# Part of a weight piece kept in a PSUM bank, a new step order, and the last stores moved off GpSimd

## The chip, the core and the metric

The kernel runs on one core of one Trainium2 chip. The core has TensorE (PE, matrix products; its weight loads are shown as PEld), VectorE (DVE), ScalarE (ACT), GpSimd (POOL) and SyncE (SP), which here only issues DMAs. The engines run side by side, each through its own instructions in order, and wait for each other through semaphores. Sixteen DMA engines move data between DRAM and the on-chip memory (SBUF). PE writes its results to PSUM, which has eight banks of 2 KB on each of 128 partitions. The metric is the device time of one execution in microseconds (us); lower is better.

## The reference

Two independent results stand side by side in the output. Part A is a sliding-window attention over 2048 rows. Part B, which takes most of the time, is a recurrence: 64 segments of 32 rows, each with 8 memory rows that the segment before has made.

```python
for s in range(n_seg):                                # 64 segments
    h = jnp.concatenate([mem, xs], axis=1)            # 8 memory rows + 32 rows, 640 wide
    q = jnp.einsum('btd,dhe->bhte', h, Wq)            # 32 heads of 192: 640 -> 6144
    k = jnp.einsum('btd,dhe->bhte', h, Wk)
    v = jnp.einsum('btd,dhe->bhte', h, Wv)
    scores = jnp.einsum('bhqe,bhke->bhqk', q, k) * scale
    p = _softmax(jnp.where(mask, scores, -1e9))
    o = jnp.einsum('bhqk,bhke->bhqe', p, v)
    o = jnp.einsum('bhte,hed->btd', o, Wo)            # 6144 -> 640
    mem = o[:, :M, :]                                 # the next segment needs this
    outs.append(o[:, M:, :])
```

The four weights of part B have 640 x 6144 numbers each, 31 MB in bf16 together, and every segment uses all of them. They do not fit into SBUF, which is why some of them are read again in each segment.

## The kernel before

Part A runs first. While it runs, SP loads those weights of part B that stay in SBUF (the resident units) and copies the others into contiguous pieces in DRAM (`copy_streamed`, the tensors `wcopy_*`).

Part B works in units. A unit of Wq, Wk or Wv, `(m, g, dc)`, serves one of four groups `g` of heads and one fifth `dc` of the 640 inputs; it has 1536 columns on 128 partitions, 384 KB. A unit of Wo, `("o", i, 0)` with i from 0 to 23, has 1280 columns, 320 KB, in four quarters of 320 columns. The table `STREAMED` names the units that are not resident. They come through `fetch`, which takes the next slot of a ring of seven (`nbuf=7`, `wstream`, the tile `t` in the profile) and lets SP issue one DMA from `wcopy_*`. SP runs through its DMAs in program order and waits for a slot until PE has used the unit that was in it, so it is as far ahead of PE as the seven slots allow.

One segment is a list of steps, `ORDER` (for the first segment `FIRST`). Steps of all engines stand in one list, and each of PE, DVE, ACT and SP executes its part of it in exactly this order:

- `q.g`, `k.g`, `v.g`: PE projects the segment (line 562; 20 matmuls, or 40 when the late rows are renewed as well, which happens to one k and one v group in each segment). The result lies in one of three banks `acc`.
- `e.q0` and so on: the result is copied to QT or KT by the engine that `EVACUATE` names for it (S is ACT, V is DVE; lines 568, 601); `T.q0`: DVE transposes it in place (572) and GpSimd fills in eight columns. `ve.g` copies v to `Vst` (615), always on ACT. QT, KT and Vst exist once.
- `S.g`: scores on PE (626) into one of the banks `px`; `sb`, `mx`, `sub`, `send`: the softmax on DVE, with the exponential on ACT (632 to 658), in that bank until `send` is done.
- `tp.g`, `PT.g`: PE transposes the probabilities into a `px` bank (665), ACT or DVE spreads them (`SPREAD`; 673, 676). `mix.g`: the product with v (689), into two `px` banks. `ot.g`: both are copied to OT (697) by the engines that `HEADS` names, and GpSimd stores the late rows' part.
- `out.g.0`, `out.g.1`: four and two units of Wo for groups 0 to 2 (714), accumulated in Y. `part` and `join` add the halves of Y (721, 726). `last`: the six units of group 3 (740). `close`: DVE writes the memory rows of the next segment and the output tile XS. `ql`, `eql`, `Tql`: the late rows' q of the next segment.
- At each step named in `STORE_AT`, SP issues one of the four stores of XS of the segment before. `ve.2` also issues the load of the next XS, and `tx` turns it.

In the profile, PE's order in a segment is q0 k0 k1 q1 S0 v0 q2 S1 k2 tp0 v1 q3 mix0 tp1 S2 k3 out0 (first part) v2 out0 (second part) mix1 S3 tp2 v3 mix2 out1 tp3 out2 mix3 last ql.

PSUM's eight banks in part B: three `acc`, four `px` and one for Y.

After the last segment, `project_late` multiplies the late rows of all segments, which GpSimd has stored as `late_o` (16 blocks of 384 KB), by Wo. It uses all eight banks as sums: first for the blocks m = 0 and 1, then for 2 and 3. `head` is the first ten resident units of Wo, `tail` the rest. SP loads `late_o` with `load_late` into the dead q units, four blocks during the last segment and the others later. `store` copies a sum to SBUF by ACT and DVE (871) and then stores eight strided row groups by SP, GpSimd and ACT in turn (876). Behind everything stands the program's end, in which each engine drains; its instructions carry the line number 986.

Of the kernel before, what the change touches and what calls it, by code (L numbers as in the profile page):

```python
# [23 lines left out]
def part_a(ctx, tc, A_x, A_wqkv, A_wo, out, ident, emit_loads):  # L24
# [241 lines left out]
    with tc.manual_schedule(engines={mybir.EngineType.PE, mybir.EngineType.DVE, mybir.EngineType.Activation}):  # L266
# [4 lines left out]
        for b in range(-1, n_blk):  # L271
# [12 lines left out]

STREAMED = {"q": ((), (), (), ()), "k": ((1, 3), (1, 2), (0, 2), (1, 3)), "v": ((0, 1, 4), (2, 4), (0, 2, 4), (0, 2)),
            "o": (8, 12, 17, 19, 23)}
PARTS = {}
# [4 lines left out]
    q.0 e.q0 T.q0 k.0 e.k0 T.k0 q.1 S.0 sb.0 e.q1 T.q1 k.1 mx.0 sub.0 e.k1 T.k1 send.0 v.0 ve.0 S.1 sb.1  # L292
    q.2 e.q2 tp.0 PT.0 T.q2 k.2 e.k2 T.k2 mx.1 sub.1 mix.0 ot.0 v.1 ve.1 send.1 S.2 sb.2 out.0.0 out.0.1
    tp.1 mx.2 sub.2 PT.1 q.3 e.q3 T.q3 k.3 send.2 e.k3 T.k3 mix.1 ot.1 v.2 ve.2 tp.2 PT.2 out.1.0 S.3
    sb.3 mx.3 sub.3 out.1.1 mix.2 ot.2 send.3 v.3 ve.3 out.2.0 tp.3 PT.3 tx out.2.1 part mix.3 ot.3 join
    ql eql last close Tql
# [12 lines left out]
LEAD_IN = 114  # L309
# [10 lines left out]
def part_b(ctx, tc, B_x, B_mem0, B_Wq, B_Wk, B_Wv, B_Wo, out, ident, n_seg, pre, nbuf, mid):  # L320
# [8 lines left out]

    def streamed(u):  # L330
        return u[1] in STREAMED["o"] if u[0] == "o" else u[2] in STREAMED[u[0]][u[1]]

# [28 lines left out]
    def quarter(w, u, i):  # L361

        n = quarter_cols(u)
        if isinstance(w, tuple):
            now = PARTS[u]
            v = w[0][:, n * i:n * i + n] if i < now else w[1][:, n * (i - now):n * (i - now) + n]
            return v.rearrange("p (b c) -> p b c", b=2) if u[0] == "o" else v
        if u[0] == "o":
            return w[:, 640 * (i // 2):640 * (i // 2) + 640].rearrange("p (b g c) -> p g b c", b=2, g=2)[:, i % 2]
        return w[:, n * i:n * i + n]  # L370

    def stream_cols(u):
        return quarter_cols(u) * PARTS.get(u, 4)

# [5 lines left out]
    def copy_streamed():  # L380

        for m, g in need:
            for u in pieces(m, g):
                if u in PARTS:
# [79 lines left out]
    ps_acc = pool("b_ps_acc", bufs=3, space=PSUM)  # L464
    ps_x = pool("b_ps_x", bufs=4, space=PSUM)
    ps_y = pool("b_ps_y", bufs=1, space=PSUM)
    respool2 = pool("b_res2", bufs=1)
    place_resident(respool2, resident[n_pre + len(early):])
    wait.update(resident[n_pre + len(early):])

    fetched = {}

    def fetch(u):
        t = wstream.tile([128, SLOT], BF16, tag="ws")
        nc.sync.dma_start(t[:, 0:stream_cols(u)], copied[u])
        return t[:, 0:stream_cols(u)]

# [280 lines left out]
    def segment(s):  # L758
# [90 lines left out]
    def project_late():  # L849
# [18 lines left out]
        def store(m):  # L868
# [5 lines left out]
            for n in range(M):  # L874
                queue = (nc.sync, nc.gpsimd, nc.scalar if m == 3 and n < 6 else nc.sync)[n % 3]
                queue.dma_start(dst[SEG - M + n], rows[n:128:M])
# [114 lines left out]
```

## Time and profile before

| what | value |
|---|---|
| median of 3 runs | 1866.58 us (1863.11 to 1874.28) |
| the profiled execution: its own time | 1876.93 us |
| its span, first to last instruction | 1875.0 us |
| mean granted TensorE clock | 0.986 |
| busy time of PE, DVE, ACT, POOL | 1649.2, 1288.8, 683.8, 556.9 us |
| moved by DMA | 627.62 MB, mean 335 GB/s |

The profile covers one execution. A group row names the line, the engine, the operation, what is written and read, the shapes and the count, then the busy time and the mean duration in ns, and then the idle time of the engine just before these instructions with what ended it. A row of the timeline has the start, the length, the engine, the line, the operation and the count; in brackets stands the idle time before it and what ended it. A row of the table of waits gives the total, the number of times and the longest. A row of the DMA issues gives the size and the median time from issue to landing. Matmuls are pipelined and their ends are modelled, so a short wait of PE can be hidden inside its busy time.

### The profile page before, as it was taken

What the parts mean: (1) busy time and instruction counts of PE and PEld (TensorE: products, weight loads), DVE (VectorE), ACT (ScalarE), POOL (GpSimd) and SP (SyncE); (2) the same over time, 40 slices, a digit from 0 to 9 for tenths busy, and PEclk for the clock granted to TensorE, in tenths of its full rate; (3) what the DMA queues carried; (4) which work ended last, traced back from release to release, by engine and by line L of the source; (5) the groups of instructions that cost most, each with busy time, mean ns of one, the idle gap of its engine ahead of it and who ended that gap; (6) DMA issues with size and microseconds to landing.
All of it is one profiled execution on the core that took longest, in us unless ns stands there. A gap on an engine that the chain in (4) does not pass through costs nothing.

```text
span 1875.0 us, 91432 instructions
## 1 busy us (share of the span) xinstructions
PE 1649.2 (88%) x39286; PEld 1043.2 (56%) x39286; DVE 1288.8 (69%) x3671; ACT 683.8 (36%) x1821; POOL 556.9 (30%) x1624
## 2 busy tenths in 40 slices
PE   8998898888998888888899889888988888899887
PEld 5565555555555555555555555555555555455567
DVE  4786676767777777776777767776777777677730
ACT  3454333333333333333333333333333333333310
POOL 3001233333333333332333333233333333333311
PEclk9998999999999999999999999999999999999999
DMA  9925999999999999999999999999999999999980
GB/s 327 321 72 196 377 358 354 351 350 360 369 368 351 365 358 363 344 362 357 343 360 366 356 347 358 358 351 344 364 354 362 354 361 351 326 366 351 353 336 24
DMA packets 277858, 627.62 MB, mean 335 GB/s; under 512 B 64116, under 2 KB 76898, under 8 KB 277452
## 3 DMA queue, kind: packets, MB, share of 16 engines
q1 hardware_dynamic: 266668, 610.37, 91.0%
q0 software_dynamic: 10720, 11.36, 1.8%
q8 instruction: 308, 5.05, 1.1%
q14 instruction: 98, 0.80, 0.1%
q10 hardware_dynamic: 64, 0.04, 0.0%
HBM read 607.47 MB, written 22.91 MB: 336 GB/s over the span
## 4 chain that ended last, share of the span: by engine, by line
PE 51%; DMA 27%; DVE 10%; issue 5%; ACT 4%; SPq 1%; POOL 0%; ACTq 0%; DVEq 0%; POOLq 0%
PE acc L562 26%; DMA t<-wcopy_v 22%; PE Y L714 6%; PE px L626 4%; PE px L740 3%; PE pq L95 3%; PE px L689 3%; DMA t<-wcopy_k 3%; PE px L863 1%; DMA t<-wcopy_o 1%; ACT OT L697 1%; PE po L161 1%; ACT QT L721 1%; PE px L665 1%; PE acc L863 1%
## 5 line engine op out<-in xcount | busy, mean ns | idle before, releaser
L562 PEld LDWEIGHTS <-HX 128*32 128x32 bf16 x19380 | 503.1, 96 | 384.0 <-issue 156.8
L562 PE MATMUL acc<-t,HX 128*32 128x384 bf16 x5812 | 434.7, 329 | 65.4 <-DMA t<-wcopy_v 43.0
L562 PE MATMUL acc<-wres_q,HX 128*32 128x384 bf16 x6460 | 324.3, 328 | 14.1 <-issue 12.3
L562 PE MATMUL acc<-wres_k,HX 128*32 128x384 bf16 x3876 | 270.6, 327 | 9.8 <-issue 8.2
L698 POOL COPY OL<-OT 128x96 bf16<-128x96 bf16 x256 | 159.5, 623 | 266.3 <-ACT OT L697 171.8
L562 PE MATMUL acc<-wres_v,HX 128*32 128x384 bf16 x3232 | 215.9, 330 | 4.0 <-issue 3.8
L697 DVE CAST OT<-px 128x240 bf16<-128x240 f32 x256 | 103.7, 405 | 165.8 <-PE px L689 147.9
L608 POOL COPY QT<-Lb 128x96 bf16<-128x96 bf16 x252 | 68.0, 270 | 473.5 <-PE px L626 472.9
L714 PE MATMUL Y<-wres_o,OT 128*32 128x320 bf16 x3840 | 192.3, 304 | 5.4 <-issue 5.3
L572 DVE STREAM_TRANSPOSE QT<-QT 128x384 bf16<-128x384 bf16 x256 | 146.6, 573 | 42.7 <-ACT QT L601 40.5
L697 ACT CAST OT<-px 128x240 bf16<-128x240 f32 x256 | 92.5, 361 | 219.5 <-PE px L689 120.4
L601 ACT CAST KT<-acc 128x384 bf16<-128x384 f32 x192 | 92.4, 481 | 217.5 <-PE px L626 170.9
L626 PE MATMUL px<-KT,QT 64*64 64x40 bf16 (+1 forms) x4096 | 138.4, 189 | 31.8 <-DVE KT L572 20.8
L615 ACT CAST Vst<-acc 128x384 bf16<-128x384 f32 x256 | 123.5, 482 | 115.4 <-PE px L689 92.1
L699 POOL DMA_DIRECT2D late_o<-OL x256 | 138.2, 540 | 77.0 <-POOL OL L698 59.6
L632 DVE SCALAR_TENSOR_TENSOR px<-px,mask 128x160 f32<-128x160 f32 x256 | 82.7, 323 | 110.0 <-PE px L626 109.6
L626 PEld LDWEIGHTS <-QT 64*64 64x64 bf16 (+1 forms) x4096 | 108.4, 109 | 88.9 <-issue 49.9
L714 PEld LDWEIGHTS <-OT 128*32 128x32 bf16 x4608 | 114.7, 97 | 57.7 <-issue 11.8
L572 DVE STREAM_TRANSPOSE KT<-KT 128x384 bf16<-128x384 bf16 x256 | 142.1, 555 | 1.7
L568 ACT CAST sb<-acc 128x384 bf16<-128x384 f32 x115 | 55.1, 479 | 235.3 <-PE acc L562 202.9
L644 ACT ACTIVATE px<-px 128x160 f32<-128x160 f32 x256 | 74.2, 290 | 147.7 <-DVE px L643 138.0
L689 PE MATMUL px<-PT,Vst 64*128 64x80 bf16 (+1 forms) x2048 | 122.6, 213 | 4.6 <-issue 2.8
(103 smaller groups left out, 2438.7 us busy)
## 6 DMA issues: line engine op xcount, KB each, us to landing
t<-wcopy_v SPq DMA_DIRECT2D x640, 384.0 KB, 5.8
t<-wcopy_k SPq DMA_DIRECT2D x512, 384.0 KB, 5.3
t<-wcopy_o SPq DMA_DIRECT2D x330, 320.0 KB, 5.9
wres_q<-in_B_Wq_dram SPq DMA_DIRECT2D x20, 384.0 KB, 7.8
late_o<-OL POOLq DMA_DIRECT2D x256, 24.0 KB, 5.2
wres_q<-late_o SPq DMA_DIRECT2D x16, 384.0 KB, 6.5
wres_o<-in_B_Wo_dram SPq DMA_DIRECT2D x19, 320.0 KB, 7.0
wres_k<-in_B_Wk_dram SPq DMA_DIRECT2D x12, 384.0 KB, 8.0
```

Source lines behind the costliest of these rows:

```text
L562: nc.tensor.matmul(ps[n][32 * j:32 * j + 32].rearrange("p (f n) -> p f n", n=32), lhsT=X[:, dc, :], rhs=columns(w, (m, g, dc), j), start=( ...
L572: nc.vector.transpose(t, t)
L601: copies[1](columns_of(m, 0, 32), ps[-1][:].rearrange("p (f n) -> p f n", n=32))
L615: S_(Vst[:], ps[-1][:])
L626: nc.tensor.matmul(Sps[64 * h:64 * h + 64, a, :], lhsT=QT[k0:k1, L * f:L * f + 64], rhs=KT[k0:k1, f, :], start=(outer == 0 and a == 0), st ...
L632: nc.vector.scalar_tensor_tensor(out=Sps, in0=Sps, scalar=scale, in1=mask[:].unsqueeze(1).to_broadcast([128, 4, L]), op0=ALU.mult, op1=ALU ...
L644: nc.scalar.activation(t1[:], t1[:], ACTF.Exp)
L689: nc.tensor.matmul(ps[r][lo:hi, 2 * L * k:2 * L * k + 2 * L], lhsT=V[64 * r:64 * r + 64, col:col + hi - lo], rhs=PT[64 * r:64 * r + 64, 2 ...
L697: copy(OT[:, 6 * r:6 * r + 6].rearrange("p c n -> p (c n)"), ps[r][:, 0:6 * L])
L698: nc.gpsimd.tensor_copy(OL[:, g % 2].rearrange("p n c -> p c n"), OT[:, :, 32:L])
L699: nc.gpsimd.dma_start(late_o[s // 4][:, g, s % 4], OL[:, g % 2].rearrange("p n c -> p (n c)"))
L714: nc.tensor.matmul(Y[t:t + 32].rearrange("p (b c) -> p b c", b=2), lhsT=OT[:, slot(c), 0:32], rhs=quarter(w, ("o", i, 0), 2 * r + gv), sta ...
```

## The change

The tables. Streamed are now ten units of Wk and eight of Wv (before eight and ten), and four of Wo instead of five. One more unit of Wo, number 21 (`HELD`), is neither resident nor wholly streamed: only its first quarter, 80 KB, is copied to `wcopy` and fetched in each segment. Its other three quarters are loaded once, by `hold()` at the start of part B, and DVE writes them as raw bits into a PSUM bank, `held`. In each segment a new step `w.0` fetches the first quarter into a ring slot, and ACT copies the 960 held columns from PSUM into the same slot; `last` then finds the whole unit there. `project_late` fetches the unit in the same way, once in each of its two passes.

The held bank is taken from `px`, which has three banks now. `ORDER`, `FIRST`, `EVACUATE`, `HEADS` and `STORE_AT` are new. PE's order is now q0 k0 q1 k1 S0 k2 S1 q2 v0 tp0 v1 q3 mix0 S2 tp1 k3 mix1 out0 (first part) v2 out0 (second part) tp2 S3 out1 mix2 v3 tp3 out2 mix3 last ql. Step `w.0` stands between `tp.3` and `PT.3`.

At the end: `project_late` starts with seven sums and takes the eighth bank in its second pass. The late blocks 0 to 7 are all loaded at its beginning, none during the last segment. The row groups are stored by SP, three of the last block's by ACT, and none by GpSimd.

```diff
-STREAMED = {"q": ((), (), (), ()), "k": ((1, 3), (1, 2), (0, 2), (1, 3)), "v": ((0, 1, 4), (2, 4), (0, 2, 4), (0, 2)),
-            "o": (8, 12, 17, 19, 23)}
+STREAMED = {"q": ((), (), (), ()), "k": ((0, 3), (1, 2), (0, 2, 4), (1, 2, 4)), "v": ((0, 4), (3, 4), (1, 3), (2, 4)),
+            "o": (6, 11, 18, 22)}
+HELD = ("o", 21, 0)
...
 ORDER = """
-    q.0 e.q0 T.q0 k.0 k.1 e.k0 T.k0 q.1 S.0 sb.0 e.k1 e.q1 mx.0 sub.0 v.0 T.q1 ve.0 T.k1 q.2 S.1 send.0
-    e.q2 T.q2 sb.1 mx.1 k.2 tp.0 v.1 e.k2 q.3 PT.0 sub.1 mix.0 T.k2 send.1 tp.1 S.2 ve.1 ot.0 sb.2 e.q3
-    PT.1 mx.2 sub.2 k.3 T.q3 send.2 out.0.0 e.k3 v.2 out.0.1 mix.1 T.k3 S.3 ot.1 tp.2 sb.3 mx.3 v.3 PT.2
-    ve.2 mix.2 sub.3 out.1.0 send.3 out.1.1 ot.2 tp.3 ve.3 out.2.0 out.2.1 part tx PT.3 mix.3 ot.3 last
-    join ql close eql Tql
+    q.0 k.0 e.q0 T.q0 q.1 e.k0 T.k0 k.1 S.0 e.q1 sb.0 e.k1 T.q1 k.2 T.k1 mx.0 sub.0 S.1 e.k2 send.0 q.2
+    e.q2 sb.1 v.0 tp.0 mx.1 sub.1 ve.0 T.q2 v.1 send.1 T.k2 q.3 PT.0 mix.0 S.2 ve.1 ot.0 sb.2 e.q3 mx.2
+    tp.1 PT.1 k.3 mix.1 out.0.0 T.q3 v.2 out.0.1 e.k3 sub.2 T.k3 send.2 ot.1 ve.2 tp.2 S.3 PT.2 out.1.0
+    out.1.1 mix.2 sb.3 mx.3 sub.3 v.3 send.3 ot.2 tp.3 w.0 PT.3 out.2.0 out.2.1 ve.3 tx mix.3 part ot.3
+    join last ql close eql Tql
 """
-EVACUATE = {"k0": "SV", "k1": "SS", "k2": "VS", "k3": "SS", "q0": "VV", "q1": "SS", "q2": "SS", "q3": "VV"}
-HEADS = ("VS", "SV", "VS", "SV")
+EVACUATE = {"k0": "SV", "k1": "SS", "k2": "VS", "k3": "SV", "q0": "VS", "q1": "VS", "q2": "VS", "q3": "SV"}
+HEADS = ("VS", "SV", "SS", "SV")
 SPREAD = "SSVV"
-STORE_AT = ("tp.0", "PT.0", "tp.1", "e.k3")
+STORE_AT = ("tp.0", "send.1", "PT.0", "T.q3")
...
-    ps_x = pool("b_ps_x", bufs=4, space=PSUM)
+    ps_x = pool("b_ps_x", bufs=3, space=PSUM)
     ps_y = pool("b_ps_y", bufs=1, space=PSUM)
+    held = pool("b_ps_w", bufs=1, space=PSUM).tile([128, 512], FP32, name="held")
...
+    def hold():
+        t = wstream.tile([128, SLOT], BF16, tag="ws")
+        load_quarters(t[:, 0:960], HELD, (1, 2, 3))
+        nc.vector.tensor_scalar(out=held[:, 0:480].bitcast(mybir.dt.uint32), in0=t[:, 0:960].bitcast(mybir.dt.uint32),
+                                scalar1=0, scalar2=None, op0=ALU.bitwise_or)
+
     def fetch(u):
         t = wstream.tile([128, SLOT], BF16, tag="ws")
         nc.sync.dma_start(t[:, 0:stream_cols(u)], copied[u])
+        if u == HELD:
+            nc.scalar.copy(t[:, 320:1280], held[:, 0:480].bitcast(BF16))
+            return t[:, 0:1280]
         return t[:, 0:stream_cols(u)]
...
-                if last and (m, g) == ("k", 3):
-                    load_late((2, 3))
...
-                elif last and g == 1:
-                    load_late((0, 1))
...
+            elif name == "w":
+                fetched[HELD] = fetch(HELD)
...
-        sums = [bank()[:] for _ in range(4)] + [acc[0][:], acc[1][:], acc[2][:], y[:]]
+        sums = [bank()[:] for _ in range(3)] + [acc[0][:], acc[1][:], acc[2][:], y[:]]
...
             for n in range(M):
-                queue = (nc.sync, nc.gpsimd, nc.scalar if m == 3 and n < 6 else nc.sync)[n % 3]
-                queue.dma_start(dst[SEG - M + n], rows[n:128:M])
+                (nc.scalar if m == 3 and n in (1, 3, 5) else nc.sync).dma_start(dst[SEG - M + n], rows[n:128:M])
...
             if first:
-                load_late((4, 5, 6, 7))
+                load_late(range(8))
+            else:
+                sums.append(bank()[:])
...
+    hold()
     fetch_first(nbuf)
```

More of the change, by code (lines that the diff above doesn't have):

```diff
@@ L292 @@
     q.0 e.q0 T.q0 k.0 e.k0 T.k0 q.1 S.0 sb.0 e.q1 T.q1 k.1 mx.0 sub.0 e.k1 T.k1 send.0 v.0 ve.0 S.1 sb.1
-    q.2 e.q2 tp.0 PT.0 T.q2 k.2 e.k2 T.k2 mx.1 sub.1 mix.0 ot.0 v.1 ve.1 send.1 S.2 sb.2 out.0.0 out.0.1
+    q.2 e.q2 tp.0 PT.0 T.q2 k.2 e.k2 T.k2 mx.1 sub.1 send.1 mix.0 ot.0 v.1 ve.1 S.2 sb.2 out.0.0 out.0.1
     tp.1 mx.2 sub.2 PT.1 q.3 e.q3 T.q3 k.3 send.2 e.k3 T.k3 mix.1 ot.1 v.2 ve.2 tp.2 PT.2 out.1.0 S.3
-    sb.3 mx.3 sub.3 out.1.1 mix.2 ot.2 send.3 v.3 ve.3 out.2.0 tp.3 PT.3 tx out.2.1 part mix.3 ot.3 join
-    ql eql last close Tql
+    sb.3 mx.3 sub.3 out.1.1 send.3 mix.2 ot.2 v.3 ve.3 out.2.0 tp.3 PT.3 tx w.0 out.2.1 part mix.3 ot.3
+    join ql eql last close Tql
 """
 ORDER = """
-    q.0 e.q0 T.q0 k.0 k.1 e.k0 T.k0 q.1 S.0 sb.0 e.k1 e.q1 mx.0 sub.0 v.0 T.q1 ve.0 T.k1 q.2 S.1 send.0
-    e.q2 T.q2 sb.1 mx.1 k.2 tp.0 v.1 e.k2 q.3 PT.0 sub.1 mix.0 T.k2 send.1 tp.1 S.2 ve.1 ot.0 sb.2 e.q3
-    PT.1 mx.2 sub.2 k.3 T.q3 send.2 out.0.0 e.k3 v.2 out.0.1 mix.1 T.k3 S.3 ot.1 tp.2 sb.3 mx.3 v.3 PT.2
-    ve.2 mix.2 sub.3 out.1.0 send.3 out.1.1 ot.2 tp.3 ve.3 out.2.0 out.2.1 part tx PT.3 mix.3 ot.3 last
-    join ql close eql Tql
-"""
-EVACUATE = {"k0": "SV", "k1": "SS", "k2": "VS", "k3": "SS", "q0": "VV", "q1": "SS", "q2": "SS", "q3": "VV"}
-HEADS = ("VS", "SV", "VS", "SV")
+    q.0 k.0 e.q0 T.q0 q.1 e.k0 T.k0 k.1 S.0 e.q1 sb.0 e.k1 T.q1 k.2 T.k1 mx.0 sub.0 S.1 e.k2 send.0 q.2
[3 more added lines that the diff above has]
+    join last ql close eql Tql
+"""
+EVACUATE = {"k0": "SV", "k1": "SS", "k2": "VS", "k3": "SV", "q0": "VS", "q1": "VS", "q2": "VS", "q3": "SV"}
+HEADS = ("VS", "SV", "SS", "SV")
 SPREAD = "SSVV"
-STORE_AT = ("tp.0", "PT.0", "tp.1", "e.k3")
+STORE_AT = ("tp.0", "send.1", "PT.0", "T.q3")
 LEAD_IN = 114
@@ L330, in streamed @@
     def streamed(u):
+        if u == HELD:
+            return True
         return u[1] in STREAMED["o"] if u[0] == "o" else u[2] in STREAMED[u[0]][u[1]]
@@ L363, in quarter @@
         n = quarter_cols(u)
+        if u == HELD:
+            return w[:, n * i:n * i + n].rearrange("p (b c) -> p b c", b=2)
         if isinstance(w, tuple):
@@ L383, in copy_streamed @@
             for u in pieces(m, g):
-                if u in PARTS:
+                if u == HELD:
+                    copied[u] = dpool.tile([128, stream_cols(u)], BF16, name="wcopy_%s%d_%d" % u)[:]
+                    load_quarters(copied[u], u, (0,))
+                elif u in PARTS:
                     copied[u] = dpool.tile([128, stream_cols(u)], BF16, name="wcopy_%s%d_%d" % u)[:]
```

3 lines of the change are left out of this document (2 added, 1 removed).

## The prediction

> **What bounds the kernel now.** I read the page first: span, DMA line, queues, DMA issues.
>
> ```profile
> span 1875.0 us, 91432 instructions
> DMA  9925999999999999999999999999999999999980
> ...
> q1 hardware_dynamic: 266668, 610.37, 91.0%
> q0 software_dynamic: 10720, 11.36, 1.8%
> ...
> t<-wcopy_v SPq DMA_DIRECT2D x640, 384.0 KB, 5.8
> t<-wcopy_k SPq DMA_DIRECT2D x512, 384.0 KB, 5.3
> t<-wcopy_o SPq DMA_DIRECT2D x330, 320.0 KB, 5.9
> ```
>
> From the fifth slice to the last two, the DMA engines are nine tenths busy or more, and nearly all of it is the weight stream: 10 units of Wv, 8 of Wk and 5 of Wo in each of 64 segments. Next, the view by stretches over 63 segments, from the first step `last` to the 64th, and the timeline rows at both ends:
>
> ```profile
> 212.11:1805.26 1593.15, 1407.11 (x35016) 872.63 (x35006) 1143.22 (x3480) 586.73 (x1622) 510.88 (x1511) 0.99 0.99 356
> ```
>
> ```profile
> 212.11 0.31 PE L740 MATMUL px<-wres_o,OT 128*32 128x160 bf16 x8
> ...
> 1805.26 0.25 PE L740 MATMUL px<-wres_o,OT 128*32 128x160 bf16 x4 [0.63 <-ACT OT L697]
> ```
>
> A segment takes 1593.15 / 63 = 25.29 us; the DMA share is 0.99 at 356 GB/s, PE is busy 22.33, DVE 18.15, ACT 9.31 and POOL 8.11 us of it. The granted clock is 0.99, so no throttle is in play. What PE waits for in this stretch, from the table of waits:
>
> ```profile
> PE acc L562 <- DMA t<-wcopy_v: 41.5, 74, 1.6
> PE px L740 <- ACT OT L697: 38.0, 63, 0.6
> ...
> PE px L626 <- DVE KT L572: 20.8, 35, 0.9
> ...
> PE acc L562 <- DMA t<-wcopy_k: 4.9, 10, 1.2
> ```
>
> So two limits lie close together. DMA: 25.04 us of packets a segment and 0.25 idle. PE without its waits for weights: 25.29 - 46.4/63 = 24.55. DMA decides now, with 0.74 us before PE's own chain takes over. PE's longest wait of its own, for ot.3 ahead of `last`, is left as it is: in both orders `part`, ot.3 and `last` follow mix.3.
>
> **The change, part by part.**
>
> *Fewer bytes.* Five units of Wo at 320 KB become four and one quarter of 80 KB, 240 KB less a segment; Wk and Wv keep 18 units together. Price of a packet by the two queue rows: q1 0.910 x 1875 us x 16 / 266668 = 102.4 ns at 2289 B, q0 50.4 ns at 1060 B. The line through both gives 113.8 ns for 2560 B and 32.6 ns for 640 B (rows of a unit of Wo and of its quarter). Saved: 128 x (113.8 - 32.6) / 16 = 0.65 us. If the short packet costs what q0's does, 0.51; if bytes alone count, 0.246 MB / 356 GB/s = 0.69. I take 0.65, the price between two measured sizes. DMA side: 25.29 - 0.65 = 24.64.
>
> *The order of a segment.* PE's order changes, so I follow what PE waits for. The old hand-over from S.0 to S.1:
>
> ```profile
> 1021.19 0.47 PE L626 MATMUL px<-KT,QT 64*64 64x40 bf16 x11 [0.19 <-issue]
> ...
> 1024.30 0.27 PE L626 MATMUL px<-KT,QT 64*64 64x40 bf16 x7 [0.42 <-DVE KT L572]
> ```
>
> ```profile
> 1021.70 0.33 DVE L632 SCALAR_TENSOR_TENSOR px<-px,mask 128x160 f32<-128x160 f32 x1 [1.77 <-PE px L626]
> 1022.07 0.33 DVE L639 TENSOR_REDUCE mx<-px 128x4 f32<-128x160 f32 x1
> 1022.43 0.33 DVE L643 TENSOR_TENSOR px<-px,mx 128x160 f32<-128x160 f32 x1
> 1022.67 0.57 DVE L572 STREAM_TRANSPOSE QT<-QT 128x384 bf16<-128x384 bf16 x1
> 1023.16 0.53 DVE L572 STREAM_TRANSPOSE sb<-sb 128x384 bf16<-128x384 bf16 x1
> 1023.62 0.53 DVE L572 STREAM_TRANSPOSE KT<-KT 128x384 bf16<-128x384 bf16 x1
> ```
>
> ```profile
> 1021.70 0.48 ACT L601 CAST KT<-acc 128x384 bf16<-128x384 f32 x1 [1.30 <-PE px L626]
> 1022.08 0.48 ACT L601 CAST QT<-acc 128x384 bf16<-128x384 f32 x1
> ```
>
> ```profile
> 1015.69 1.86 PE L562 MATMUL acc<-wres_q,HX 128*32 128x384 bf16 x40
> 1017.38 0.34 PE L562 MATMUL acc<-wres_k,HX 128*32 128x384 bf16 x4
> ```
>
> QT and KT are single, so e.q1 and e.k1 cannot start before S.0 has ended (1021.66). Old chain, when k1 is not renewed (no transpose of sb): sb, mx, sub, T.q1, T.k1 and 0.15 until PE goes, 2.18 us; PE has v.0 and q.2 in between, 20 matmuls each at 1.69/2 = 0.845, so it waits 0.49. New chain: DVE does only sb before T.q1, which waits for e.q1 (0.53); two transposes (0.49, 0.53) and 0.15 give 1.70; PE has only k.2, 0.845, so it waits 0.85 in two of four segments, 1.31 where k1 is renewed, nothing where k2 is (its 40 matmuls take 1.69). Mean 0.75; the old one is 0.49, 0.49, 0.95, 0: 0.48, of which 20.8/63 = 0.33 is seen, the rest being swallowed by waits for weights. Plus 0.27.
>
> *Three small banks.* With tp.2 in one, S.3 needs one that ot.1 empties, and ot.1 writes OT only when out.0.1 has read it. After out.0.1: ACT's copy 0.36 (row below) and two hand-overs of 0.05 against tp.2's 0.24 (the rows below: 1039.30 to 1039.54): plus 0.22. tp.3 is nearer to S.3 now, but ot.2 no longer stands on DVE ahead of out.2.0. What that place hides today:
>
> ```profile
> 1038.37 0.46 PE L714 MATMUL Y<-wres_o,OT 128*32 128x320 bf16 x8
> ...
> 1039.30 0.28 PE L665 MATMUL px<-ident,P 128*128 128x128 bf16 x2
> 1039.54 0.32 PE L714 MATMUL Y<-t,OT 128*32 128x320 bf16 x4
> ...
> 1061.55 0.46 PE L714 MATMUL Y<-wres_o,OT 128*32 128x320 bf16 x8
> ...
> 1062.78 0.28 PE L665 MATMUL px<-ident,P 128*128 128x128 bf16 x2
> ```
>
> The same 24 matmuls take 0.93 us and, where PE waits for P, 1.23: 0.30 inside busy time, to be won at best. So the order costs PE between -0.30 and +0.49 + 0.30 (two more bank hand-overs like S.3's, at mix.0 and tp.1, minus the cover they have). I take +0.3: nearest to the two chains that I could follow to the end (0.49), less part of what is hidden.
>
> *The held copy on ACT.* Rows for its price, from the groups (busy, mean ns):
>
> ```profile
> L601 ACT CAST KT<-acc 128x384 bf16<-128x384 f32 x192 | 92.4, 481 | 217.5 <-PE px L626 170.9 <-PE acc L562 45.8 <-DVE px L632 0.9
> L697 ACT CAST OT<-px 128x240 bf16<-128x240 f32 x256 | 92.5, 361 | 219.5 <-PE px L689 120.4 <-PE Y L714 92.3 <-PE px L626 5.2
> ```
>
> (481 - 361) / 144 = 0.833 ns a column, so 960 columns take 481 + 576 x 0.833 = 961 ns. Behind it on ACT stand ve.3, part and ot.3. From mix.2's end ACT needs two ot.2 (0.36 and, overlapped, 0.26), the copy 0.96 and ve.3 0.48: 2.06. PE has v.3 0.845, tp.3 0.24 and out.2 0.93 before mix.3, which needs ve.3: 2.02. I cost it at nothing; where that cover goes, each 0.1 us of delay is 0.1 us a segment. ACT grows from 9.3 to about 10.6 us a segment and DVE loses a 0.4 us cast: neither becomes the bound. The slot is no issue: its last user, seven fetches back, is in k.3.
>
> *Steps moved with their queues.* The four stores and the load of XS stay on SP, the load now two fetches behind the last store instead of five. With weights landing 5.3 to 5.9 us after issue, about five units are under way, so SP can stand still for 2 us without emptying the engines: 0, at worst +0.1 a segment. The first segment's two earlier `send` steps: 0.
>
> The segment is the larger side. PE 24.55 + 0.30 = 24.85, DMA 24.64: I take 24.85, a gain of 0.44 x 63 = 27.7 us.
>
> *Start.* hold() adds three loads of 80 KB in 320 B rows, 768 packets: 0.9 us of DMA by the line above, and one DVE operation, which needs a bank that part A uses to its end.
>
> ```profile
> 177.68 0.56 DVE L568 CAST sb<-acc 128x384 bf16<-128x384 f32 x1 [6.63 <-PE acc L562]
> ...
> 165.06 0.38 SPq L407 DMA_DIRECT2D wres_o<-in_B_Wo_dram  x1
> 179.01 0.33 SPq L475 DMA_DIRECT2D t<-wcopy_v  x1
> ```
>
> (The timelines of DVE and SP.) DVE is idle for 6.63 us and SP for 13.6 just there. The seventh fetch now waits for that operation, and the nine early resident loads may stand behind it: 0 to +5 us; I take +0.5.
>
> *End.* Rows after the last computation, from the timeline of SP, the view of the kernel's last line, the stretches (the eighth column is the granted clock, the last two DMA share and GB/s) and the DMA issues:
>
> ```profile
> 1862.76 1.76 SPq L876 DMA_DIRECT2D out_dram<-wres_q  x3
> ...
> L986 POOLq DRAIN x3: 46/102/10130, 1864.1 to 1874.7; - x3
> ...
> 1866.50:1875.00 8.50, 0.00 (x0) 0.00 (x0) 0.00 (x0) 0.00 (x0) 0.00 (x0) 0.55 0.00 0
> ...
> out_dram<-wres_q SPq DMA_DIRECT2D x18, 20.0 KB, 2.4
> ```
>
> For 8.5 us nothing moves: GpSimd drains for 10.13 us after its last store. Its last DMA will now be the last segment's four stores, so that drain passes under the 55 us of late projection. SP issues five rows of the last block instead of three, at 0.59: the fifth starts at 1862.76 + 4 x 0.59 = 1865.1 and lands at 1867.5; with the 0.8 us that now follow the drain, the span ends at 1868.3: -6.7. The late loads move: four leave the last segment, eight stand together behind its fetches. Nobody moves more bytes, but PE needs the first four at once: 0, bounded by four units, +-4. The eighth sum bank waits for the first store, covered by the head's ten units.
>
> The Trainium skill (Trainium Kernel Development and Optimization, Key Constraints) says that DMAs from the SP, ACT and POOL queues run on the same 16 engines and that issuing from several only saves issue time. By that rule the end would grow by SP's two more issues, +1.2 us, and the sum would be 8 us less gain; the drain row says otherwise, so the rule stands as the third rival.
>
> *Sum.* The profiled execution took 1876.93 us (span 1875.0). -27.7 - 6.7 + 0.5 = -33.9: 1843.0. It stood 10.35 over the median of the three runs, 1866.58; taken off that median: 1832.7, rounded to 1833.
>
> **The rivals.** First, PE's chain takes all that DMA gives: the order's upper end, +0.79, makes the segment 25.34, +3.2 us, against -6.2 for end and start: 1863.6. For it: the two limits are 0.74 apart; against: part of every new wait falls where PE waits for weights today. Second, slower: the three banks. If mix.0, tp.1, mix.1 and S.3 each wait as S.3 does (0.22) with nothing swallowed, and S.1's 0.27 comes on top, PE's side is 24.55 + 1.15 = 25.70, +26 - 6.2: 1886. Nothing is left of the gain once the banks and S.1 together cost over 0.84, and it is slower by 0.5% from 0.99. Against: ot.0 and PT.0 are done while PE has k.3 or v.1 to run. Third, GpSimd's drain is not what holds the end: +1.2 there, 1840.6.
>
> **How the numbers follow.** 0.5% (9 us) is about what a measurement can tell here, the three runs being 11 apart. Forecast 0.69 (its own range 1814 to 1850: DMA's full 0.69 x 63 with 8 for the end, to half of the gain); first rival 0.13, of which 0.03 falls short of its upper end and under 1857, 0.10 is the same; second 0.12; third 0.06, still faster. Faster 0.78, same 0.10, slower 0.12. Range 1814 to 1864: 0.12 is above it and some 0.03 below.
>
> **What would show it.** A segment near 24.85; t<-wcopy_o issues of 80 KB; PE's wait for t<-wcopy_v down to a third; PE L626 waiting for KT about twice as long, and S.3 for ACT's OT; some 66 copies of 0.96 us on ACT; the last DRAIN of GpSimd gone from the end. Wrong if waits for weights stay and segments shorten by less than 0.2, or if mix.3 waits for Vst.

## The result, and the profile after

The changed kernel takes 1942.97 us, median of 5 runs (1937.07 to 1952.48), against 1866.58 before: 1.038 times as long, with a 95% interval of 1.034 to 1.043. Predicted were 1833 and a range that ended at 1864. The direction was wrong.

First the page of the changed kernel: span, DMA in 40 slices, the hardware queue that carries the weights, and the issues of the small piece.

```profile
span 1950.7 us, 91482 instructions
...
DMA  9927999999999999999999999999999999999991
...
q1 hardware_dynamic: 267836, 594.37, 87.1%
...
t<-wcopy_o SPq DMA_DIRECT2D x66, 80.0 KB, 4.5
```

The bytes are fewer, as planned: 594.37 MB on this queue against 610.37. The page's slices hide what is wrong, since each is 49 us long, nearly two segments. The same stretch as before, from the first step `last` to the 64th (timeline rows, then the stretch; its last three columns are granted clock, DMA share and GB/s):

```profile
209.83 0.32 PE L758 MATMUL px<-t,OT 128*32 128x160 bf16 x8
...
1884.42 0.32 PE L758 MATMUL px<-t,OT 128*32 128x160 bf16 x8 [0.63 <-ACT OT L715]
```

```profile
209.83:1884.42 1674.59, 1435.29 (x35008) 883.99 (x35008) 1122.77 (x3416) 669.65 (x1749) 515.63 (x1511) 0.97 0.94 329
```

A segment takes 1674.59 / 63 = 26.58 us instead of 25.29: +81.4 us over 63. The time up to the first `last` is 2.3 us shorter, the time behind the 64th 3.5 us shorter (66.3 against 69.7). The sum, +75.6, is the difference of the two profiled executions (1952.48 and 1876.93 us). So the whole loss lies in the segments, and there DMA is no longer full: 0.94 instead of 0.99. What PE waits for, and what SP waits for (the DMA queue's own waits):

```profile
PE acc L580 <- DMA t<-wcopy_v: 75.1, 106, 2.8
PE Y L732 <- DMA t<-wcopy_o: 41.6, 50, 2.1
PE px L758 <- ACT OT L715: 38.6, 63, 0.8
PE acc L580 <- DMA t<-wcopy_k: 22.3, 44, 1.4
PE px L644 <- DVE KT L590: 19.6, 33, 0.8
```

```profile
SPq L553 <- DMA out_dram<-XS: 180.6, 62, 4.3
...
SPq L490 <- DVE held L485: 12.1, 1, 12.1
```

The same wait of SP in the kernel before:

```profile
SPq L535 <- DMA out_dram<-XS: 32.9, 40, 2.0
```

PE waits for weights although fewer are sent: 139 us instead of 46. And SP, which has to issue them, stands at line 553, the load of the next XS, in 62 of 63 segments, 2.9 us each. XS is one tile for both directions: the next input may not be written into it before the last of the four stores of the old output has read it. The timelines of SP, first after, then before (x2 is two DMAs in a row):

```profile
1045.44 0.40 SPq L790 DMA_DIRECT2D out_dram<-XS  x1
1046.06 1.26 SPq L490 DMA_DIRECT2D t<-wcopy_v  x2
1051.64 0.32 SPq L553 DMA_DIRECT2D XS<-xwindows  x1
1052.01 1.03 SPq L490 DMA_DIRECT2D t<-wcopy_o  x2
```

```profile
1024.72 0.33 SPq L774 DMA_DIRECT2D out_dram<-XS  x1
1025.14 2.89 SPq L475 DMA_DIRECT2D t<-wcopy_v  x5
1028.12 0.74 SPq L535 DMA_DIRECT2D XS<-xwindows  x1
```

After, SP issues two fetches behind the store and then nothing from 1047.32 to 1051.64. The store holds 7.5 KB, yet the load behind it goes out 6.2 us later. The trace's DMA packets say why: the store is issued at 1045.44, but its 24 rows move between 1048.6 and 1050.9, after 321 rows of weights that start in between (a unit has 128). While SP stands, the engines have nothing behind the store but the two fetches, and when SP goes on these are nearly through as well: of their 256 rows 19 start after 1051.64. The DMA engines over the 11 us from 1045 to 1056, in 40 slices of 0.275 us:

```profile
DMA  9777999778899799999999621112568589998997
```

From 1051.3 on they run nearly empty for 1.4 us (five slices), and they are full again two microseconds after SP's first new fetch. The price is seen a little later. The stretches behind it, with the same columns as above:

```profile
1047.00:1050.00 3.00, 2.29 (x61) 1.33 (x53) 2.24 (x8) 2.00 (x6) 0.00 (x0) 1.00 0.91 329
1050.00:1053.00 3.00, 3.00 (x75) 1.98 (x79) 2.47 (x7) 0.92 (x4) 1.57 (x4) 1.00 0.54 198
...
1056.00:1059.00 3.00, 1.85 (x45) 0.92 (x37) 1.55 (x6) 1.77 (x4) 1.26 (x4) 1.00 1.00 348
1059.00:1062.00 3.00, 2.03 (x46) 1.21 (x45) 0.94 (x3) 0.95 (x3) 0.61 (x2) 0.89 1.03 408
1062.00:1065.00 3.00, 2.49 (x72) 2.01 (x68) 1.91 (x7) 0.47 (x2) 1.15 (x2) 0.54 0.94 333
```

DMA falls to 0.54 first. PE, fed by the slots already filled, works on until 1056, then has 1.15 and 0.97 us without work, and in the next 3 us its granted clock is 0.54. The longest of these pauses is a wait for a unit of Wv:

```profile
1059.97 0.35 PE L580 MATMUL acc<-t,HX 128*32 128x384 bf16 x4 [1.88 <-DMA t<-wcopy_v]
```

### The profile page after: what moved, and what is told of

It is laid out like the page before. It is cut to its first block, busy times and chain, and to the rows that moved or that the text cites. A ratio compares the mean times of both kernels' runs of the same rounds, so it can differ in the third digit from the quotient of the medians.

```text
span 1950.7 us, 91482 instructions
## 1 busy us (share of the span) xinstructions
PE 1676.0 (86%) x39286; PEld 1054.7 (54%) x39286; DVE 1269.3 (65%) x3609; ACT 769.4 (39%) x1950; POOL 555.9 (28%) x1612
## 3 DMA queue, kind: packets, MB, share of 16 engines
q1 hardware_dynamic: 267836, 594.37, 87.1%
## 4 chain that ended last, share of the span: by engine, by line
PE 50%; DMA 38%; DVE 5%; ACT 3%; issue 2%; SPq 1%; POOL 0%; DVEq 0%; ACTq 0%
PE acc L580 26%; DMA t<-wcopy_v 23%; DMA t<-wcopy_k 8%; PE Y L732 5%; DMA t<-wcopy_o 4%; PE px L758 3%; PE pq L95 3%; PE px L707 3%; PE px L644 2%; PE px L683 2%; PE px L879 1%; PE po L161 1%; ACT OT L715 1%; ACT QT L739 1%; PE acc L879 1%
## 5 line engine op out<-in xcount | busy, mean ns | idle before, releaser
L580 PE MATMUL acc<-t,HX 128*32 128x384 bf16 x5816 | 426.0, 332 | 117.3 <-DMA t<-wcopy_v 75.1
L580 PE MATMUL acc<-wres_q,HX 128*32 128x384 bf16 x6460 | 319.4, 329 | 4.2 <-issue 2.4
L580 PE MATMUL acc<-wres_v,HX 128*32 128x384 bf16 x3876 | 246.6, 338 | 0.4 <-issue 0.4
L580 PE MATMUL acc<-wres_k,HX 128*32 128x384 bf16 x3228 | 227.3, 327 | 1.1 <-issue 0.5
L619 ACT CAST QT<-acc 128x384 bf16<-128x384 f32 x192 | 92.0, 479 | 219.3 <-PE px L644 162.4
L694 DVE TENSOR_TENSOR PT<-px,own 128x320 bf16<-128x320 f32 x128 | 62.5, 488 | 157.0 <-PE px L683 156.8
L715 DVE CAST OT<-px 128x240 bf16<-128x240 f32 x192 | 78.1, 407 | 132.1 <-PE px L707 98.6
L644 PE MATMUL px<-KT,QT 64*64 64x40 bf16 (+1 forms) x4096 | 137.9, 189 | 23.1 <-DVE KT L590 19.6
L715 ACT CAST OT<-px 128x240 bf16<-128x240 f32 x320 | 109.6, 363 | 53.8 <-PE px L707 50.0
```

The costliest lines, as they stand in the source:

```text
L580: nc.tensor.matmul(ps[n][32 * j:32 * j + 32].rearrange("p (f n) -> p f n", n=32), lhsT=X[:, dc, :], rhs=columns(w, (m, g, dc), j), start=( ...
L619: copies[1](columns_of(m, 0, 32), ps[-1][:].rearrange("p (f n) -> p f n", n=32))
L644: nc.tensor.matmul(Sps[64 * h:64 * h + 64, a, :], lhsT=QT[k0:k1, L * f:L * f + 64], rhs=KT[k0:k1, f, :], start=(outer == 0 and a == 0), st ...
L715: copy(OT[:, 6 * r:6 * r + 6].rearrange("p c n -> p (c n)"), ps[r][:, 0:6 * L])
```

## The experiments

The theory: SP's wait at the load of XS empties the DMA queue, and the place of the load, two fetches behind the last store, is the whole loss. The rivals: the third small bank, the copy on ACT, the order of the steps, or the short packets of the held piece. Each line of the table is one kernel; "segment" is from the one profiled execution and so carries its scatter, the ratio (95% interval) is against runs of the kernel before on the same chip. The medians come from several chips, on which the kernel before takes 1867 to 1878 us, so kernels are compared by the ratios.

| kernel | median us | ratio | segment us | SP's wait at the load, us |
|---|---|---|---|---|
| changed kernel | 1942.97 | 1.0383 (1.0341 to 1.0425) | 26.58 | 180.6 |
| e1 load later | 1863.09 | 0.9927 (0.9893 to 0.9961) | 24.98 | under 1 |
| e3 before, load at once | 2120.16 | 1.1283 (1.1215 to 1.1352) | 28.99 | 253.3 |
| e4 before, end's stores | 1870.22 | 0.9957 (0.9922 to 0.9992) | 25.35 | 35.1 |
| e5 e1 without held piece | 1876.44 | 1.0010 (0.9980 to 1.0041) | 25.50 | under 1 |
| e6 store earlier | 1883.69 | 1.0026 (0.9997 to 1.0056) | 25.43 | 4.4 |
| e7 e5 with four banks | 1869.31 | 0.9959 (0.9930 to 0.9989) | 25.38 | 0.4 |
| e8 before, held piece | 1897.88 | 1.0104 (1.0068 to 1.0140) | 25.66 | 37.7 |
| e9 e1, late loads early | 1862.07 | 0.9924 (0.9896 to 0.9951) | 25.17 | 2.5 |
| e10 stores by ACT | 2024.04 | 1.0786 (1.0729 to 1.0843) | 27.85 | 247.5 |
| e11 three fetches between | 1881.61 | 1.0027 (1.0004 to 1.0049) | 25.51 | 131.0 |
| e12 e9, stores by ACT | 1865.20 | 0.9945 (0.9908 to 0.9983) | 25.22 | 22.9 |
| e13 e8, copy moved | 1885.20 | 1.0054 (1.0019 to 1.0089) | 25.34 | 37.5 |

### The load moved away from the store (e1)

```diff
-                if g == 2:
-                    load_x(s + 1)
...
                 got["v", g] = values(s, g)
+                if g == 3:
+                    load_x(s + 1)
```

Six fetches now stand between the last store and the load.

> The changed kernel, with one edit: SP issues the load of the next XS behind the two fetches of v.3 instead of at ve.2, so that six weight fetches stand between the last store of XS and this load instead of two. Theory A (SP stands behind the stores' landing, and a store lands only after the weights queued ahead of it, so the DMA engines run dry): SP's wait for out_dram at the load falls from 180.6 us to under 40, the DMA share of the steady stretch returns from 0.94 to 0.98 or more, a segment falls from 26.58 us to 24.7 to 25.0, and the time to 1830 to 1850. Rival B (the weights themselves come slower in this order, 123 ns for a packet of Wo instead of 110, or three banks and the copy on ACT hold PE): the segment stays over 26 us and the time over 1910.

1863.09 us. The stretch over the 63 segments, and PE's wait for Wv:

```profile
212.28:1785.85 1573.57, 1398.59 (x35008) 868.15 (x35008) 1123.32 (x3416) 664.59 (x1749) 515.84 (x1511) 0.99 0.99 350
```

```profile
PE acc L580 <- DMA t<-wcopy_v: 27.0, 46, 3.3
```

One moved load takes some 80 us off, and the changed kernel becomes 0.7% faster than the kernel before. The time is above the expected 1830 to 1850, and far from the rival's 1910. The profiled execution was one of the two fastest (1854.2 us); its segment of 24.98 us is 0.13 above the 24.85 that was predicted. DMA is full again.

### The kernel before, with the load directly behind the store (e3)

```diff
                 nc.sync.dma_start(*stores.pop(0))
+                if (name,) + at == ("e", "k3"):
+                    load_x(s + 1)
...
-                if g == 2:
-                    load_x(s + 1)
-                elif last and g == 1:
+                if last and g == 1:
```

> The kernel before, with the load of the next XS issued directly behind the last store (at e.k3) instead of at ve.2: no weight fetch between them instead of five. Nothing else is touched. Theory A: SP waits 4 to 6 us in each segment for the store to land, 250 to 380 us in all instead of 32.9, and the kernel becomes slower by 70 to 160 us (1935 to 2025). Rival B: the wait of SP is hidden by the five units under way; within 10 us of 1867.

```profile
SPq L535 <- DMA out_dram<-XS: 253.3, 94, 5.8
```

```profile
211.57:2038.03 1826.46, 1491.46 (x35015) 884.80 (x35005) 1142.74 (x3480) 586.32 (x1622) 509.29 (x1511) 0.93 0.88 311
```

The old kernel, with nothing else changed, loses 12.8%: 28.99 us a segment, 3.7 more. So the loss needs none of the change's other parts. It is larger than the expected 1935 to 2025 us. With no fetch between store and load it is the full price of starting the stream again, slower matmuls included: PE's busy time grows from 1407.11 to 1491.46 us.

### Only the stores at the end (e4)

```diff
-                queue = (nc.sync, nc.gpsimd, nc.scalar if m == 3 and n < 6 else nc.sync)[n % 3]
-                queue.dma_start(dst[SEG - M + n], rows[n:128:M])
+                (nc.scalar if m == 3 and n in (1, 3, 5) else nc.sync).dma_start(dst[SEG - M + n], rows[n:128:M])
```

> The kernel before, with only the last stores changed: SP and, for three of the last block's rows, ACT; none by GpSimd. From the prediction's step: the end falls from 10.3 us behind the last store's issue to about 3.5, -6.7 us (1860). The rule that several issuing engines only save issue time: +1.2 us.

0.43% faster, 8 us by the ratio (interval 1.5 to 14.6). In the profiled executions the time behind the 64th `last` falls from 69.7 to 63.6 us. The last line's instructions on GpSimd (minimum, median and longest duration in ns, then when the first and the last begin):

```profile
L985 POOLq DRAIN x3: 46/102/9458, 1814.0 to 1872.9; - x3
```

The long drain now begins at 1814.0 and is over long before the end. In the kernel before it began at 1864.1. This part of the change does what it was predicted to do.

### Without the held piece (e5), and with the bank given back (e7)

e5 is e1 with unit 21 streamed whole, in its `w.0` step, and no copy on ACT; the bank that held it stays unused. e7 gives that bank back to the small ones.

```diff
-            "o": (6, 11, 18, 22)}
-HELD = ("o", 21, 0)
+            "o": (6, 11, 18, 21, 22)}
+HELD = None
```

```diff
-    ps_x = pool("b_ps_x", bufs=3, space=PSUM)
+    ps_x = pool("b_ps_x", bufs=4, space=PSUM)
```

> As e1_load_later, but unit 21 of Wo is streamed whole (320 KB, five full units), so there is no held bank in use, no copy on ACT and no 80 KB fetch; the order and the three small banks stay. If the DMA engines bound e1_load_later, this one is slower than it by 0.65 us a segment, 41 us (1870 to 1890). If PE or ACT bound it, the two are within 10 us, or this one is faster because ACT has 0.96 us less to do before ve.3.

> The new order with the load behind v.3, unit 21 of Wo streamed whole, and the bank that then holds nothing given back, so that there are four small banks; beside the run with the same bytes and three banks (1876.4, 25.50 us a segment). Theory (DMA decides, and the third bank costs PE nothing that shows): 1868 to 1884, 25.3 to 25.5 a segment. Rival (three banks cost PE 0.2 us a segment or more at mix.0, tp.1 and S.3): 1864 or less, 25.3 or less, and the waits of PE for OT in tp and S shrink.

```profile
212.43:1819.21 1606.78, 1410.60 (x35015) 871.65 (x35004) 1124.79 (x3416) 614.38 (x1685) 514.99 (x1511) 0.99 0.99 352
```

```profile
212.48:1811.12 1598.64, 1409.50 (x35016) 867.57 (x35005) 1126.94 (x3416) 608.78 (x1685) 514.89 (x1511) 0.99 0.99 354
```

The held piece is worth 1606.78 less 1573.57, 33 us, in the profiled executions, and 13 us in the medians, 0.2 to 0.5 us a segment. The lower figure is the better one, since e1's profiled execution was among its fastest and e5's (1886.17 us) among its slowest. It is neither the 41 us of the theory nor quite within the rival's 10. The third bank costs 8 us in the profiled executions and 0.4 to 0.5% by medians and ratios, about 0.13 us a segment, somewhat more than the theory's nothing and less than the rival's 0.2; the two ratios' intervals just overlap. With three banks PE waits at `tp` for the bank that DVE's copy to OT empties, 8.9 us in 44 segments of e5 and 9.6 us in 46 of e1; with four, in e7, 1.7 us in 2. Part of that only changes place, since PE's wait for P at `tp` is 12.0 us in e7 and 8.3 in e5, so what the rest of the 0.13 us is stays open. With four banks and every byte streamed, e7 is as fast as e4 (0.9959 and 0.9957): the new order by itself brings nothing.

### The store moved instead of the load (e6)

```diff
-STORE_AT = ("tp.0", "send.1", "PT.0", "T.q3")
+STORE_AT = ("tp.0", "send.1", "PT.0", "tp.1")
```

> The changed kernel with its load of XS where it was, and only the last of the four stores earlier, from T.q3 to tp.1, so that five fetches stand between that store and the load instead of two. Theory (SP stands still at the load until the store has landed, and the fetches behind it are late): SP's wait for out_dram at the load falls from 180.6 us to some 33, as in the kernel before with its five fetches, the DMA share in the steady stretch is back from 0.94 to 0.98 or more, a segment takes 25.0 to 25.4 us instead of 26.58, the time is 1863 to 1885. Rival (the load's own place at ve.2 or the new order of the fetches costs the time): the time stays above 1920.

```profile
SPq L553 <- DMA out_dram<-XS: 4.4, 17, 0.8
```

```profile
1062.52 2.62 SPq L790 DMA_DIRECT2D out_dram<-XS  x3
```

The load stands where the change put it, and 59 of the 80 us are back: not its place, but its distance from the store counts. 1883.69 lies inside the expected range, the segment (25.43) just above it. It is still 1% behind e1. In its timeline three stores now stand in a row, and no fetch is issued for 2.62 us in this segment. PE's wait for Wk, of which k.3's three fetches come behind these stores, is 41.8 us in all and was 17.2 in e1; that this is the remaining 1% was not tested.

### Three fetches between store and load (e11)

The load moves behind `out.1.0`, so that one unit of Wo more lies between.

```diff
                 project_out(got["Y"], g, range(4 * half, 4 + 2 * half))
+                if (g, half) == (1, 0):
+                    load_x(s + 1)
```

> The changed kernel with the load moved from ve.2 to behind out.1.0, so that three fetches (two of Wv, one of Wo) stand between the last store and the load, instead of two. Theory: when the store has landed, only the fetches behind it are still under way; they cover 1.1 us each (0.9 for a unit of Wo) of a loss that is 3.7 us where there are none (29.0 less 25.3 us a segment in the run with the load directly behind the store). Two cover 2.2, leaving 1.5, and 26.58 less 24.98 is 1.6; three cover 3.1 and leave 0.6: 25.6 a segment, 1880 to 1910. Rival (it was the place ve.2 of the load, ahead of the fetch of unit 6, that cost the time): the time of the run with the load behind v.3, 1863.

```profile
211.02:1818.37 1607.35, 1410.81 (x35016) 872.05 (x35004) 1123.58 (x3417) 666.10 (x1749) 515.22 (x1511) 0.99 0.97 342
```

```profile
SPq L553 <- DMA out_dram<-XS: 131.0, 61, 3.8
```

1881.61 us, inside the expected range and not the 1863 of the rival. What is left, 0.3 us a segment by the ratios and 0.5 in the profiled executions, is a little less than the expected 0.6. SP still stands 2.1 us in nearly every segment, but that alone is cheap now: the DMA share is 0.97. The loss against the case with no such wait, worked out as the difference of ratios times 1875 / 63, falls with the number of fetches in between:

| fetches between | kernels compared | loss, us a segment |
|---|---|---|
| 0 | e3 against the kernel before | 3.8 |
| 2 | changed kernel against e1 | 1.4 |
| 3 | e11 against e1 | 0.3 |

Each fetch in between saves about 1.1 to 1.2 us, roughly the time that its bytes take (at 350 GB/s, 1.1 us for 384 KB and 0.9 for the third fetch's 320 KB), until nothing is left to lose.

### The stores through ACT's queue (e10, e12)

```diff
-STORE_AT = ("tp.0", "send.1", "PT.0", "T.q3")
+STORE_AT = ("k.1", "k.2", "v.0", "v.1")
...
-                nc.sync.dma_start(*stores.pop(0))
+                nc.scalar.dma_start(*stores.pop(0))
```

e10 does this to the changed kernel, e12 to e9.

> The changed kernel with its load of XS where it was, and the four stores of a segment issued by ACT at k.1, k.2, v.0 and v.1, so on another queue than the weights and earlier. Theory (what costs is SP standing until a store has landed that lies behind the weights in SP's own queue): SP's wait for out_dram at the load falls from 180.6 to under 10 us, the DMA share is 0.98 again, 1855 to 1885. First rival (a store of another queue lands as late, since the same engines carry it): SP's wait stays over 100 us, over 1920. Second rival (four issues of some 0.6 us hold ACT's copies and exponentials up): PE's waits for ACT grow by 0.4 us a segment or more, over 1888 with SP's wait gone.

> The load behind v.3, half of the late blocks loaded in the last segment, and the four stores issued by ACT at k.1, k.2, v.0 and v.1. Theory (SP's four issues of 0.4 us each are small gaps in the stream of weights, as the run with the earlier store shows where three stand in a row): DMA share 0.99, 24.8 us a segment, 1846 to 1860. Rival (ACT's issues delay its copies, which PE waits for): 1866 or more, with PE's waits for ACT grown.

```profile
SPq L553 <- DMA out_dram<-XS: 247.5, 63, 5.6
```

```profile
1066.82 0.31 ACTq L790 DMA_DIRECT2D out_dram<-XS  x1
1067.84 0.32 SPq L490 DMA_DIRECT2D t<-wcopy_v  x1
1071.74 0.32 SPq L553 DMA_DIRECT2D XS<-xwindows  x1
```

My expectation failed, and the first rival holds: e10 takes 2024.04 us, 4% more than the changed kernel. Two things show in the rows. The store goes out on another queue at 1066.82 and SP may load at 1071.74, 4.9 us later. Over 62 segments the mean is 4.8 us, against 5.2 through SP's queue in the changed kernel: the other queue is hardly quicker. And the store goes out late. SP issues several fetches ahead of what PE is doing, while ACT issues the store when it has itself come to v.1. Of v.2's two fetches SP has issued the first at 1064.96; only the second, at 1067.84, comes behind the store, and in 34 of the 62 segments none does. The loss against e1, worked out as in the table, is 2.6 us a segment, between the rows for none and for two. I had looked at the list of steps and forgotten that the engines do not stand at the same place in it. In e12, with the load four fetches later, the wait is 22.9 us in all, and nothing is gained or lost against e9 (0.9945 and 0.9924). So the gaps that single stores leave among SP's fetches, which e12's theory blamed, cost nothing that shows.

### The late blocks loaded during the last segment again (e9)

```diff
+                if last and (m, g) == ("k", 3):
+                    load_late((2, 3))
...
+                if last and g == 1:
+                    load_late((0, 1))
...
-                load_late(range(8))
+                load_late((4, 5, 6, 7))
```

> The run with the load behind v.3 (1863.1), and four of the eight late blocks loaded in the last segment again. Theory (eight blocks at the start of the late projection make PE wait there; from the last segment's last step to the end the kernel before with the end's stores moved took 63.6 us, this one 66.4): 63.6 there, 1860. Rival (the late loads only move a wait, and the last segment is longer by as much): no difference from the start of the last segment to the end, 1863.

No difference: 0.9924 against 0.9927. By the timelines, from the 64th `last` to the end it is 63.9 us instead of 66.4, as the theory said, but the segment ahead of it takes 29.98 instead of 25.48, as the rival said.

### The held piece in the old order (e8, e13)

e8 is the kernel before with the held piece and three small banks, nothing else; e13 moves the copy.

```diff
-            "o": (8, 12, 17, 19, 23)}
+            "o": (8, 12, 17, 19)}
+HELD = ("o", 23, 0)
...
-    ve.2 mix.2 sub.3 out.1.0 send.3 out.1.1 ot.2 tp.3 ve.3 out.2.0 out.2.1 part tx PT.3 mix.3 ot.3 last
+    ve.2 mix.2 sub.3 out.1.0 send.3 out.1.1 ot.2 tp.3 ve.3 w.0 out.2.0 out.2.1 part tx PT.3 mix.3 ot.3 last
...
-    ps_x = pool("b_ps_x", bufs=4, space=PSUM)
+    ps_x = pool("b_ps_x", bufs=3, space=PSUM)
```

```diff
-    ve.2 mix.2 sub.3 out.1.0 send.3 out.1.1 ot.2 tp.3 ve.3 w.0 out.2.0 out.2.1 part tx PT.3 mix.3 ot.3 last
+    ve.2 mix.2 sub.3 w.0 out.1.0 send.3 out.1.1 ot.2 tp.3 ve.3 out.2.0 out.2.1 part tx PT.3 mix.3 ot.3 last
```

> The kernel before with the held piece alone: unit 23 of Wo in a quarter that is streamed and three that are held, three small banks, w.0 behind ve.3; order, placement of stores and load, the end and the late loads as before. Theory (DMA decides and the bytes are its price, 0.5 to 0.65 us a segment, of which PE lets 0.4 through): 24.9 us a segment, 1843 to 1858. Rival (the old order needs its fourth bank, each S and mix waits for one): 25.3 a segment or more, 1870 or more.

> The run with the held piece alone in the old order, with step w.0 moved from behind ve.3 to behind sub.3, where ACT idles ahead of ot.2. In the run with w.0 behind ve.3 ACT works without a gap from ot.2 to ot.3 and the copy of 0.99 us lies in that chain: PE waits 1.0 us a segment for ot.3 ahead of the last step instead of 0.6. Theory (this is 0.4 us of the loss, and the missing fourth bank, seen as 0.27 us a segment of PE at S.3 waiting for OT, is the rest): 25.66 - 0.4 = 25.26 a segment, 1868 to 1880, the wait at S.3 still there. Rival (the bank decides): 25.6, 1890 or more.

PE's waits and ACT's timeline in e8, then PE's waits in e13:

```profile
PE px L758 <- ACT OT L715: 63.3, 63, 1.4
...
PE px L644 <- DVE OT L715: 17.9, 48, 0.5
```

```profile
1053.31 0.48 ACT L633 CAST Vst<-acc 128x384 bf16<-128x384 f32 x1
1053.68 0.50 ACT L635 CAST Lv<-acc 128x384 bf16<-128x384 f32 x1
1054.05 0.99 ACT L492 COPY t<-held 128x960 bf16<-128x960 bf16 x1
1055.07 0.59 ACT L739 COPY QT<-Y 64x160 f32<-64x160 f32 x2
1055.68 0.36 ACT L715 CAST OT<-px 128x240 bf16<-128x240 f32 x1
```

```profile
PE px L758 <- ACT OT L715: 38.4, 63, 0.8
...
PE px L644 <- DVE OT L715: 16.2, 48, 0.5
```

With the same bytes saved as in e1, e8 is 1.0% slower than the kernel before, and lies in its rival's range. ACT works without a gap from ve.3 to ot.3, and the copy lies in that chain: PE waits 1.0 us a segment for ot.3 instead of 0.6. Moved to a place where ACT idles, the copy costs nothing (0.61), and e13 gains back 0.5% (the two intervals overlap a little), less than expected (1885 against 1868 to 1880). What stays is S.3 waiting for DVE's ot.1, 16.2 / 63 = 0.26 us a segment, which I put down to the missing fourth bank; no run separates it. In the new order S.3 has no such wait, and the one for ot.3 is as short as before (38.9 us in e1); the wait at `tp`, 0.15 us a segment, stands in their place. Compared alike, with the bank's price included, the held piece costs 0.5% in the old order even with its copy moved (e13 against the kernel before) and gains 0.3% in the new one (e1 against e7), which the intervals do not separate from nothing. So what the new order brings is room for the held piece, and not much more.

## Why the prediction was wrong, point by point

- **What bounds the kernel.** Right: DMA decides, and PE's own chain lies just below. In the changed kernel DMA idles 6% of 26.58 us, 1.6 us a segment, where it was 0.25 before, and e1 brings it back to 0.25.
- **Fewer bytes, 0.65 us a segment.** The price on the DMA side is nearly right: in e1's packets a row of 640 B takes 36 ns and one of 2560 B 109, which makes 128 x 73 / 16 = 0.58 us. The segment got shorter by only 0.2 to 0.5 between e5 and e1.
- **The order, +0.27 at S.1 and +0.22 at S.3.** Neither shows. S.1's wait for KT is 19.6 / 63 = 0.31 us a segment, where it was 0.33, and S.3 does not wait for OT in the new order. The wait for a bank stands at `tp` instead, 9.5 / 63 = 0.15 us a segment in the changed kernel, and the third bank costs about 0.13.
- **The held copy on ACT at nothing.** Right for this order. Predicted were 961 ns; the groups of the changed kernel show 978:

```profile
L492 ACT COPY t<-held 128x960 bf16<-128x960 bf16 x66 | 64.6, 978 | 19.9 <-PE acc L879 19.9
```

- **Steps moved with their queues: "SP can stand still for 2 us without emptying the engines: 0, at worst +0.1 a segment". This is the step that failed.** The distance was seen, two fetches instead of five, and costed as a stand of a given length against a full queue. But the stand is 2.9 us long, and the queue is not full in it: what SP waits for is a store whose rows move behind the fetches issued before it. From then until new fetches flow, the engines have only the fetches issued behind the store, two units or 2.2 us, and e3 shows 3.7 to 3.8 us as the cost where there are none. 3.8 less 2.2 is 1.6 us a segment; measured were 1.6 in the profiled executions and 1.4 by the ratios. The row of SP's own wait in the kernel before (32.9 us, 40 times) was there to be read: with five fetches between, the wait was already a regular one.
- **Start, +0.5.** SP did wait 12.1 us for the held bank once, with no loss: the first `last` came 2.3 us earlier, in e1 0.2 later.
- **End, -6.7.** Right in size. Counted from the 63rd `last`, so that the late loads lie in both, the rows below give 98.16 us before and 91.34 after, -6.8; e4 gave 8 us by its ratio. First the timeline of the kernel before, then that of the changed one, and its drain on GpSimd:

```profile
1776.84 0.32 PE L740 MATMUL px<-wres_o,OT 128*32 128x160 bf16 x8 [0.63 <-ACT OT L697]
```

```profile
1859.36 0.32 PE L758 MATMUL px<-t,OT 128*32 128x160 bf16 x8 [0.63 <-ACT OT L715]
```

```profile
L1004 POOLq DRAIN x3: 46/102/9347, 1888.3 to 1950.4; - x3
```

- **The rivals.** The first did not happen. The second, three banks, got the direction for a reason that the changed kernel hardly shows (0.13 of the 1.15 us that it added up); in the old order S.3 does wait (e8, e13). The third falls with e4. None of the three had SP standing at the load, so the 0.12 for a slower kernel stood on the wrong mechanism.

The best versions, e1 and e9, are 0.7 to 0.8% faster than the kernel before, of which the end's stores alone bring 0.4 (e4), and about 4% faster than the change as it was made. A tile of its own for the next input would remove the dependence altogether; it was not tried, and no run shows whether SBUF has room for one.

## What to carry to other kernels

Where an engine that feeds a DMA stream has to wait for one of its own transfers, count the transfers that it has issued behind that one: in this kernel they were all that the DMA engines had until the engine could issue again, however full the queue was. Read every issuing engine's own waits before moving its steps, and count distances in issues of that engine, not in steps of a list that the engines pass at different times. A piece of work that needs a bank or an engine's time must find its place in the order first: the same held piece loses 1.0% in one order, half of that with its copy moved, and in the other about pays for its bank.

## What the runs showed of the hardware that was not expected

**A starved PE also runs slower afterwards.** In the stretches above the granted clock is 0.54 for the 3 us behind PE's pauses. Over the 63 segments the same 35008 matmuls keep PE busy for 1435.29 us in the changed kernel and 1398.59 in e1, 0.58 us a segment more; how much of the lost 1.6 us that is, is not shown, since part of it may lie under other waits. The trace's clock record has half speed for 92 us of the changed kernel's 63 segments and for 20 us of e1's. In e3 the mean clock falls to 0.93, with 1491.46 us busy. The Trainium skill (TensorE: Matmul & The Clock Gate, Part 1) says that the clock is halved by default and after an idle window of about 3.4 us, and that activity of that length releases it; the 0.54 behind the pauses agrees with the halving. The length does not: the longest pause ahead of it is 1.88 us, so here shorter pauses were enough.

**A store of another queue lands hardly earlier.** In e10 the 7.5 KB store of ACT's queue held SP's load up for 4.9 us, although the weights ahead of it were on SP's queue. The Trainium skill (DMA: Bandwidth & Descriptors, Queues, rings and completion order) says that a DMA's completion is written only after every earlier write of the same DMA engine, across its queues. That agrees with e10, but most of the wait passes before such a rule can matter: by the trace's packets, the 48 rows of the last two stores themselves move only between 1068.2 and 1071.0, up to 4.2 us behind the last issue, and SP goes on 0.8 us later.
